# A section with its own semaphores: ending it with a NoOp on GpSimd in place of a drain

## The chip, the cores and the metric

The kernel runs on 1 core of one Trainium2 chip. The metric is device time in microseconds (us) of one execution. Kernels that are compared were run in turns on the same chip. Spans and records are of one profiled execution; a run's time is 1.7 to 1.9 us longer than its profiled span in most runs.

The views name the engines PE (TensorE's matrix products), PEld (its weight loads), DVE (VectorE), ACT (ScalarE), POOL (GpSimd) and SP (SyncE); a q after the name means the engine's queue. A semaphore is a counter that one engine increments and another waits for. A drain and a NoOp compute nothing; at the end of the section each waits for one semaphore and then increments another as its answer. They differ in what else they wait for.

## The reference, cut to what matters

One decoded token goes through attention over a long cache and, beside it, through a small feed-forward block; a gate mixes the two.

```python
def reference(A_x, A_k_cache, A_v_cache, A_wq, A_wo, B_x, B_w_gate, B_w_up, B_w_down, gate_w):
    # attention: H=32 heads, 65536 cached positions, head size 128, one query
    q = (A_x @ A_wq).reshape(...)
    p = softmax(einsum("bhqd,bhkd->bhqk", q, A_k_cache) * 128 ** -0.5)
    a = einsum("bhqk,bhkd->bhqd", p, A_v_cache).reshape(...) @ A_wo
    b = (silu(B_x @ B_w_gate) * (B_x @ B_w_up)) @ B_w_down
    g = sigmoid((A_x * gate_w).sum(-1, keepdims=True))
    return g * a + (1 - g) * b
```

K and V together are 2 x 32 x 65536 x 128 values of 2 bytes, or 1074 MB. The page below counts 1088 MB read, so nearly all of the traffic is the cache, read once.

## The kernel before

The kernel records every operation in a plan. The plan works out which semaphore values each operation must wait for. All of it is then emitted inside one section in which the kernel handles its own semaphores. The framework puts a hand-over at the end of this section: SP says that it is over, every engine answers, and SP waits for the answers.

```python
    # all that the kernel has GpSimd ("POOL") do, in the first microseconds
    # (lines for DVE between these, and the body of select, left out):
    op("POOL", "ones_b", lambda: nc.gpsimd.memset(ones_b, 1.0), writes=["ones_b"])
    select("ident", ident, ones_b, "ones_b", [[-1, P]], 1)
    select("pick", pick, ones[0:VB, 0:VB], "ones", [[-1, VB]], 1)
    op("POOL", "sel1", lambda: nc.gpsimd.memset(sel, 1.0), writes=["sel"])
    select("sel", sel, sel, "sel", [[-1, RP], [1, P]], -RP)
    # ... 32 heads: stream K and V, products on DVE, sums and P*V on PE ...
    # the last operations:
    dve("out_sb", lambda: nc.vector.scalar_tensor_tensor(...), ["m_x", "gval", "rest4"], ["out_sb"])
    dma("out", out[0, 0].rearrange("(i p) -> i p", p=P), out_sb, ["out"], ["out_sb"])
    op("SP", "end", None, reads=["out"])          # SP waits until the output has landed

    with tc.tile_critical():                       # the section with own semaphores
        # ... one semaphore for each engine and each transfer ...
        for engine in ("SP", "ACT", "POOL", "DVE"):
            for o in plan.ops:
                if o.engine == engine:
                    put(o, o.waits)                # wait, emit, increment
        # ... the same for PE, with a loop over the heads ...
```

The softmax here doesn't subtract the row's maximum and nothing guards it: scores larger than these inputs give would overflow.

## Time and profile before

The time before was 2518.3 us (median of three runs, 2518.23 to 2518.3).

| What | Before | How to read it |
|---|---|---|
| Profiled span | 2516.4 us | from the first to the last instruction |
| Read from HBM | 1088 MB, 432 GB/s | over the whole span |
| DMA slices at 90% or more | 39 of 40 | a busy transfer stream is the limit |
| GpSimd busy | 1.9 us, 9 instructions (four are of the framework) | the last is over at 2.89 us |
| From SP's "section is over" to the start of the last instruction | 1.061 us | the only stretch that the change can touch |

These lines are of the page of the kernel before: the span, the busy time of each engine with its share of the span and the number of its instructions, the busy tenths of the DMA engines and their GB/s in 40 equal slices, and the engines on the chain that ended last. The line of DMA packets gives the bytes and the mean rate.

```profile
span 2516.4 us, 15594 instructions
PE 1977.2 (79%) x9185; PEld 410.9 (16%) x5221; DVE 1268.3 (50%) x287; ACT 99.1 (4%) x402; POOL 1.9 (0%) x9
DMA  9999999999999999999999999999999999999998
GB/s 423 433 433 432 434 435 433 438 433 434 433 433 433 434 435 435 435 433 433 433 433 435 434 433 432 435 436 434 435 433 433 433 433 435 434 436 433 434 433 376
DMA packets 20478, 1088.02 MB, mean 432 GB/s; under 512 B 2282, under 2 KB 2412, under 8 KB 2668
DMA 47%; PE 39%; DVE 13%; ACT 0%; issue 0%; another core or an unknown queue 0%; SPq 0%
```

The chain names PE for 39% of the span, but the DMA engines are busy at the same time. A buffer that PE frees lets the next transfer be issued (SP, which issues the transfers, waited 64 times for PE to finish S_ps, 1418 us in all), and the transfers already queued keep the engines full meanwhile. The Trainium skill ("DMA: Bandwidth & Descriptors", section "Where 436 GB/s comes from") puts the ceiling of the ports at 435.2 GB/s. The table by stretches agrees: 434 GB/s in the long middle. (Single slices of the page reach 438, because it counts a packet in the slice where it starts. With the bytes of each packet spread over its own time, no slice of this trace is over 434.2.) The table's columns are the stretch and its length, the busy time of each engine, the granted TensorE clock, the DMA share and the GB/s.

```profile
100.00:2400.00 2300.00, 1829.38 (x7902) 364.04 (x4217) 1166.65 (x239) 88.08 (x360) 0.00 (x0) 0.91 1.00 434
2470.00:2512.00 42.00, 36.59 (x381) 13.22 (x319) 20.43 (x10) 3.48 (x13) 0.00 (x0) 0.83 0.94 401
2512.00:2516.40 4.40, 1.22 (x20) 0.76 (x19) 0.57 (x2) 0.00 (x0) 0.00 (x0) 0.50 0.00 0
```

The fifth busy figure, GpSimd's, is zero from 100 us on. The last 4.4 us move no data in bulk, and the change acts in there. The chain in order of time shows what leads up to them (start, length, what; steps of 0.05 us and less, and one of PE of 0.25 us, are left out):

```profile
2470.97 40.88 DMA slot_65<-in_A_v_cache_dram
2511.89 0.51 PE m_c L257 x13
2512.68 0.24 DVE Z L601
2512.96 0.60 PE m_x L257 x4
2513.59 0.34 DVE out_sb L613
```

After out_sb comes the store of 1 KB, issued at 2513.95; SP sees it landed at 2515.15. The hand-over follows. Drains and semaphore instructions are not counted as busy, but the view of one source line lists them. This is the line of the section (L626), with the number of instructions, their shortest, median and longest duration in ns, and the starts of the first and the last:

```profile
L626 SPq EVENT_SEMAPHORE  x3: 17/28/28, 2515.3 to 2515.6; - x3
L626 SPq NOP  x2: 13/16/18, 0.8 to 2515.6; - x2
L626 ACTq DRAIN  x1: 8/8/8, 2515.4 to 2515.4; - x1
L626 POOLq DRAIN  x1: 41/41/41, 2515.4 to 2515.4; - x1
L626 DVEq DRAIN  x1: 17/17/17, 2515.4 to 2515.4; - x1
L626 PEldq DRAIN  x1: 8/8/8, 2515.4 to 2515.4; - x1
L626 SPq DRAIN  x1: 7/7/7, 2515.4 to 2515.4; - x1
```

The raw records of the same trace give the order to the nanosecond (start and duration in ns from the first instruction; comments added):

```
2515326   17  SP      EVENT_SEMAPHORE   "the section is over"
2515364    8  ACT     DRAIN             answers
2515368   41  GpSimd  DRAIN             answers  <- what the change replaces
2515371   17  DVE     DRAIN             answers
2515372    8  PE      DRAIN             answers
2515418    7  SP      DRAIN             answers
2515476   34  GpSimd  DRAIN             the first of its three in the final barrier
2515497   28  SP      EVENT_SEMAPHORE   waits for DVE and PE
2515571   28  SP      EVENT_SEMAPHORE   waits for SP and ACT
2515643   18  SP      NOP               waits for GpSimd
2515723    7  SP      DRAIN             barrier: ready
2515787    7  SP      DRAIN             barrier: answers GpSimd
2515819   17  GpSimd  EVENT_SEMAPHORE   barrier: all have answered
2515898   17  GpSimd  EVENT_SEMAPHORE   releases the others
2515978   64  GpSimd  DRAIN             second half of the barrier
2516072   71  GpSimd  EVENT_SEMAPHORE_RANGE_CLEAR
2516100    8  PE      DRAIN             the last answer of the other engines
2516177   34  GpSimd  DRAIN
2516255   17  GpSimd  EVENT_SEMAPHORE   all have answered
2516333   17  GpSimd  EVENT_SEMAPHORE   releases the others
2516387   51  PE      EVENT_SEMAPHORE   the last instruction
```

(In the barrier, the other records of SP, ACT, DVE and PE are left out.) GpSimd has answered at 2515.409 (2515.368 + 0.041), and SP starts the instruction that waits for it at 2515.643: 234 ns to spare. A second GpSimd drain follows for the final barrier. And in the barrier's second half GpSimd comes last: the other engines have all answered by 2516.108, while GpSimd still drains at 2516.177 and releases them at 2516.333.

### The profile page before, as it was taken

To read this page: it belongs to the slowest core of one execution; us is meant where nothing else is said; L and a number is where in the kernel's file an instruction comes from. 1 tells how busy PE (TensorE), PEld (TensorE's weight loads), DVE (VectorE), ACT (ScalarE), POOL (GpSimd) and SP (SyncE) were. 2 spreads that over 40 slices of the span, in tenths; PEclk is the share of its full clock that TensorE was granted. 3 is DMA by queue.
4 is the path that set the end of the run, shared out by engine and by line. 5 is a ranking of instruction groups with operands and counts; after the bars stand their busy time and mean duration, and the time that the engine had idled before them with its cause. 6 is when DMAs were issued, how large, how long until landed. Compare 5 with 4: busy or idle time off the path is not lost.

```text
span 2516.4 us, 15594 instructions
## 1 busy us (share of the span) xinstructions
PE 1977.2 (79%) x9185; PEld 410.9 (16%) x5221; DVE 1268.3 (50%) x287; ACT 99.1 (4%) x402; POOL 1.9 (0%) x9
## 2 busy tenths in 40 slices
PE   4687877877778778778787787787877877877788
PEld 2111111111111111111111111111111111111113
DVE  3455355464553554645545546445455364464554
ACT  0000000000000000000000000000000000000000
POOL 0000000000000000000000000000000000000000
PEclk9888989989989989898898898998989989989898
DMA  9999999999999999999999999999999999999998
GB/s 423 433 433 432 434 435 433 438 433 434 433 433 433 434 435 435 435 433 433 433 433 435 434 433 432 435 436 434 435 433 433 433 433 435 434 436 433 434 433 376
DMA packets 20478, 1088.02 MB, mean 432 GB/s; under 512 B 2282, under 2 KB 2412, under 8 KB 2668
## 3 DMA queue, kind: packets, MB, share of 16 engines
q1 hardware_dynamic: 20456, 1087.78, 99.8%
q8 instruction: 12, 0.20, 0.0%
q14 instruction: 6, 0.05, 0.0%
q10 hardware_dynamic: 4, 0.00, 0.0%
HBM read 1087.77 MB, written 0.00 MB: 432 GB/s over the span
## 4 chain that ended last, share of the span: by engine, by line
DMA 47%; PE 39%; DVE 13%; ACT 0%; issue 0%; another core or an unknown queue 0%; SPq 0%
PE O_ps L257 17%; DMA slot_67<-in_A_k_cache_dram 16%; DMA slot_66<-in_A_k_cache_dram 15%; DMA slot_65<-in_A_k_cache_dram 14%; PE S_ps_103 L275 11%; PE S_ps_104 L275 9%; DVE slot_67 L344 4%; DVE slot_66 L344 4%; DVE slot_65 L344 3%; DMA slot_65<-in_A_v_cache_dram 2%; PE m_c L257 2%; DVE S_sb_82 L369 2%; PE S_ps_103 L285 1%; ACT P_sb_83 L294 0%; PE S_ps_104 L285 0%
## 5 line engine op out<-in xcount | busy, mean ns | idle before, releaser
L344 DVE TENSOR_TENSOR slot_67<-slot_67,q_bc_79 128x16384 bf16<-128x16384 bf16 (+1 forms) x28 | 208.2, 7469 | 145.4 <-DMA slot_67<-in_A_k_cache_dram 145.4
L369 DVE TENSOR_REDUCE S_sb_82<-S_ps_104 128x128 f32<-128x1024 f32 (+1 forms) x66 | 78.7, 1192 | 395.0 <-PE S_ps_104 L275 395.0
L344 DVE TENSOR_TENSOR slot_65<-slot_65,q_bc_78 128x16384 bf16<-128x16384 bf16 x22 | 190.2, 8688 | 140.5 <-DMA slot_65<-in_A_k_cache_dram 140.5
L344 DVE TENSOR_TENSOR slot_66<-slot_66,q_bc_78 128x16384 bf16<-128x16384 bf16 x22 | 190.3, 8689 | 120.1 <-DMA slot_66<-in_A_k_cache_dram 120.1
L344 DVE TENSOR_TENSOR slot_65<-slot_65,q_bc_79 128x16384 bf16<-128x16384 bf16 x20 | 172.9, 8688 | 120.0 <-DMA slot_65<-in_A_k_cache_dram 120.0
L344 DVE TENSOR_TENSOR slot_66<-slot_66,q_bc_79 128x16384 bf16<-128x16384 bf16 x20 | 172.9, 8688 | 119.2 <-DMA slot_66<-in_A_k_cache_dram 119.2
L344 DVE TENSOR_TENSOR slot_67<-slot_67,q_bc_78 128x16384 bf16<-128x16384 bf16 x20 | 172.9, 8688 | 119.2 <-DMA slot_67<-in_A_k_cache_dram 119.2
L275 PE MATMUL S_ps_103<-slot_67,ident 128*128 128x512 bf16 x680 | 193.8, 455 | 0.0
L275 PE MATMUL S_ps_103<-slot_65,ident 128*128 128x512 bf16 x651 | 186.1, 456 | 0.0
L275 PE MATMUL S_ps_103<-slot_66,ident 128*128 128x512 bf16 x651 | 183.5, 452 | 0.0
L257 PE MATMUL O_ps<-slot_67,P_sb_83 128*4 128x512 bf16 x704 | 153.7, 379 | 21.0 <-ACT P_sb_83 L294 18.3
L257 PE MATMUL O_ps<-slot_66,P_sb_84 128*4 128x512 bf16 x704 | 153.7, 379 | 19.3 <-ACT P_sb_84 L294 19.3
L257 PE MATMUL O_ps<-slot_65,P_sb_84 128*4 128x512 bf16 x640 | 139.7, 379 | 18.3 <-ACT P_sb_84 L294 18.3
L257 PE MATMUL O_ps<-slot_67,P_sb_84 128*4 128x512 bf16 x640 | 139.7, 379 | 18.3 <-ACT P_sb_84 L294 18.3
L257 PE MATMUL O_ps<-slot_65,P_sb_83 128*4 128x512 bf16 x640 | 139.7, 379 | 18.3 <-ACT P_sb_83 L294 18.3
L257 PE MATMUL O_ps<-slot_66,P_sb_83 128*4 128x512 bf16 x640 | 139.8, 379 | 17.5 <-ACT P_sb_83 L294 17.5
L275 PE MATMUL S_ps_104<-slot_67,ident 128*128 128x512 bf16 x680 | 150.7, 379 | 0.0
L275 PE MATMUL S_ps_104<-slot_66,ident 128*128 128x512 bf16 x651 | 143.9, 379 | 0.0
L275 PE MATMUL S_ps_104<-slot_65,ident 128*128 128x512 bf16 x651 | 143.9, 379 | 0.0
L285 PE MATMUL S_ps_103<-slot_65,ident 128*128 128x512 bf16 x21 | 12.8, 608 | 138.0 <-DVE slot_65 L344 138.0
L285 PE MATMUL S_ps_103<-slot_66,ident 128*128 128x512 bf16 x21 | 12.8, 608 | 131.0 <-DVE slot_66 L344 131.0
L285 PE MATMUL S_ps_103<-slot_67,ident 128*128 128x512 bf16 x24 | 13.9, 579 | 125.6 <-DVE slot_67 L344 125.6
(100 smaller groups left out, 720.4 us busy)
## 6 DMA issues: line engine op xcount, KB each, us to landing
slot_66<-in_A_k_cache_dram SPq DMA_DIRECT2D x2, 4096.0 KB, 34.9
slot_67<-in_A_k_cache_dram SPq DMA_DIRECT2D x4, 2048.0 KB, 30.3
slot_65<-in_A_wq_dram SPq DMA_DIRECT2D x1, 4096.0 KB, 12.2
slot_66<-in_A_wo_dram SPq DMA_DIRECT2D x1, 4096.0 KB, 32.4
slot_65<-in_A_v_cache_dram SPq DMA_DIRECT2D x1, 4096.0 KB, 37.1
slot_65<-in_A_v_cache_dram SPq DMA_DIRECT2D x1, 2048.0 KB, 40.3
slot_65<-in_B_w_gate_dram SPq DMA_DIRECT2D x1, 1792.0 KB, 16.0
slot_65<-in_B_w_up_dram SPq DMA_DIRECT2D x1, 1792.0 KB, 21.0
```

The costliest lines, as they stand in the source:

```text
L257: ins = nc.tensor.matmul(out_ap, lhsT=a, rhs=b, start=start and i == 0, stop=stop and i == len(pairs) - 1,)
L275: ins = nc.tensor.add_instruction(mybir.InstMatmult(name=nc.get_next_instruction_name(), engine=mybir.EngineType.PE, ins=[nc.tensor.lower_ ...
L285: ins = nc.tensor.matmul(out_ap, lhsT=a, rhs=b, start=first, stop=last)
L344: "products", lambda: nc.vector.tensor_tensor(out=w, in0=w, in1=q_rep, op=ALU.mult),
L369: lambda: nc.vector.tensor_reduce(out=S_sb[b][:, :m], in_=S_ps[r][:, :m, :], axis=AXIS.X, op=ALU.add),
```

## The change

The intent is to end the section sooner by not draining GpSimd, which has long been idle.

```diff
-    with tc.tile_critical():
+    with tc.tile_critical(no_gpsimd_drain=True):
```

The whole difference between the two programs is one instruction of GpSimd:

```diff
-Pool Drain   waits for SP's signal   increments GpSimd's answer
+Pool NoOp    waits for SP's signal   increments GpSimd's answer
```

## The prediction

> **What bounds the kernel now.** It reads 1088 MB of HBM at a mean of 432 GB/s; the page's slices show the 16 DMA engines 90% busy or more in 39 of 40. The table by stretches gives DMA shares of 0.94 to 1.00 up to 2512 us and 0.00 for the last 4.4 us. PE (1977 us busy, 79%), DVE (1268 us, 50%) and ACT (99 us) have slack. GpSimd is busy 1.9 us in all: nine instructions, the last of which starts at 2.27 us, takes 0.62 us and is over by 2.89 us. So the time is the stream of K and V, plus a tail: in the chain of waits the last piece of V lands at 2511.84 us; out_sb is done at 2513.93; the store's issue starts at 2513.95.
>
> **What the change does.** The order of instructions shows PE, DVE, ACT and SP the same. On GpSimd one Drain becomes one NoOp in the block after the section, with the same wait (SP's signal that the section is over) and the same increment; the listing hides drains, so there it looks like an added instruction. No buffer, transfer or earlier wait moves. SP still waits for the NoOp, and the final barrier keeps its own GpSimd drains.
>
> **What it costs.** The trace's records (drains are kept there, though not counted as busy) give the end, in us:
> - 2515.326 SP signals that the section is over (17 ns);
> - 2515.364 to 2515.372 ACT, GpSimd, DVE, PE start their drains: 8, 41, 17 and 8 ns; SP's at 2515.418, 7 ns;
> - 2515.497 and 2515.571 SP's waits for DVE and PE, then SP and ACT, 28 ns each;
> - 2515.643 SP's NoOp that waits for GpSimd, 18 ns;
> - 2515.723 to 2516.44 the final barrier, twice.
>
> GpSimd's drain ends at 2515.409, 0.23 us before SP starts the instruction that waits for it. A NoOp took 13 and 18 ns on SP; on GpSimd I estimate 15 to 35 ns, by the 17 to 34 ns of its semaphore and drain records, so 5 to 25 ns are saved there. SP takes about 0.075 us for each of its three waits and sets the pace, so none of it lies on the chain. GpSimd's next drain may start some 0.02 us earlier, but the barrier waits for SP, which comes at 2515.787.
>
> The Trainium skill ("PSUM — Partial Sum Buffer", section "Engine vs sequencer instructions") says that a nop waits only until earlier instructions are dispatched, a drain until the engine is fully idle. That would matter only with GpSimd work in flight at the end; this trace shows none after 2.89 us of 2516.4.
>
> **Prediction.** 2518.3 us, unchanged; best guess of the difference 0.00 us, 0.1 us at most. The range is the repeat scatter (0.07 us in three runs, 2518.14 in the profiled one) widened for other rounds: 2517.4 to 2519.1. Faster by over 2%: 0.003; within 2%: 0.994; slower by over 2%: 0.003.
>
> **What would show it.** At the section's end GpSimd has a NOP where the drain was; SP's NoOp that waits for it starts about 0.32 us after SP's signal, as before; from that signal to the last instruction's start 1.06 us, as before, within 0.05; GB/s, DMA slices and busy times unchanged.
>
> **What would make it wrong.** A GpSimd drain that holds up the others in a way the records don't show (the tail shrinks, by under 1 us); a different granted clock (now 0.908) or HBM throughput in the other runs: 0.1% of it is 2.5 us, more than the change can be; a changed layout of the program, which I don't expect because the number of instructions is the same.

## The result, and the profile after

The changed kernel took 2518.21 us (median of six runs, 2518.06 to 2518.78) and the kernel before 2518.28 us (six runs, 2518.08 to 2519.59). Ratios here are the mean time of one kernel's fast runs over that of the other's of the same rounds, so not quite the ratio of the medians. This one is 0.9999, with a 95% interval of 0.9986 to 1.0012: the same.

The page after, the same six lines:

```profile
span 2516.4 us, 15594 instructions
PE 1974.0 (78%) x9185; PEld 410.9 (16%) x5221; DVE 1268.1 (50%) x287; ACT 99.0 (4%) x402; POOL 1.9 (0%) x9
DMA  9999999999999999999999999999999999999998
GB/s 423 433 433 432 434 433 433 439 435 433 433 433 433 433 433 436 438 434 433 433 433 434 434 433 434 433 435 439 433 434 434 433 433 433 434 435 436 433 433 377
DMA packets 20478, 1088.02 MB, mean 432 GB/s; under 512 B 2282, under 2 KB 2412, under 8 KB 2668
DMA 47%; PE 39%; DVE 13%; ACT 0%; issue 0%; another core or an unknown queue 0%; SPq 0%
```

The span, the number of instructions and the DMA slices are the same. PE's busy time differs by 3 us of 1977 while the span does not, which fits that PE is not the limit. The stretches of the table agree too:

```profile
100.00:2400.00 2300.00, 1827.49 (x7910) 364.43 (x4222) 1167.18 (x239) 88.10 (x360) 0.00 (x0) 0.91 1.00 434
2512.00:2516.40 4.40, 1.16 (x20) 0.79 (x20) 0.57 (x2) 0.00 (x0) 0.00 (x0) 0.50 0.00 0
```

In the view of the section's line, GpSimd now shows a NOP of 13 ns where the drain of 41 ns was (the first four lines; the other three show the same durations as before):

```profile
L626 SPq EVENT_SEMAPHORE  x3: 17/28/28, 2515.3 to 2515.5; - x3
L626 SPq NOP  x2: 13/16/18, 0.8 to 2515.6; - x2
L626 ACTq DRAIN  x1: 8/8/8, 2515.3 to 2515.3; - x1
L626 POOLq NOP  x1: 13/13/13, 2515.3 to 2515.3; - x1
```

The raw records, each start counted in ns from SP's signal in its own trace:

```
                                           before   after
GpSimd answers: start                        42       42
GpSimd answers: duration                     41       13
GpSimd's next drain (barrier): start        150      119
GpSimd's next drain (barrier): duration      34       41
SP's NOP that waits for GpSimd: start       317      317
the last instruction: start                1061     1061
```

GpSimd is done 28 ns sooner and comes to its next drain 31 ns sooner. SP comes to its NOP at the same nanosecond, and the end is the same to the nanosecond.

### The profile page after: what moved, and what is told of

Its sections match the earlier page's. It is cut to its first block, busy times and chain, and to the rows that moved or that the text cites. A ratio compares the mean times of both kernels' runs of the same rounds, so it can differ in the third digit from the quotient of the medians.

```text
span 2516.4 us, 15594 instructions
## 1 busy us (share of the span) xinstructions
PE 1974.0 (78%) x9185; PEld 410.9 (16%) x5221; DVE 1268.1 (50%) x287; ACT 99.0 (4%) x402; POOL 1.9 (0%) x9
## 4 chain that ended last, share of the span: by engine, by line
DMA 47%; PE 39%; DVE 13%; ACT 0%; issue 0%; another core or an unknown queue 0%; SPq 0%
DMA slot<-in_A_k_cache_dram 46%; PE S_ps L275 19%; PE O_ps L257 17%; DVE slot L344 11%; DMA slot<-in_A_v_cache_dram 2%; DVE S_sb L369 2%; PE m_c L257 1%; PE S_ps L285 1%; ACT P_sb L294 0%; SPq L181 0%; PE m_sp L257 0%; PE m_x L257 0%; DVE out_sb L613 0%; DVE Z L601 0%
## 5 line engine op out<-in xcount | busy, mean ns | idle before, releaser
L344 DVE TENSOR_TENSOR slot<-slot,q_bc 128x16384 bf16<-128x16384 bf16 (+1 forms) x132 | 1107.6, 8430 | 767.3 <-DMA slot<-in_A_k_cache_dram 767.3
L275 PE MATMUL S_ps<-slot,ident 128*128 128x512 bf16 x3964 | 998.5, 416 | 0.0
L257 PE MATMUL O_ps<-slot,P_sb 128*4 128x512 bf16 x3968 | 867.8, 379 | 113.3 <-ACT P_sb L294 109.8
L257 PEld LDWEIGHTS O_ps<-slot,P_sb 128*4 128x4 bf16 x3968 | 332.4, 85 | 1055.0 <-issue 357.3
L369 DVE TENSOR_REDUCE S_sb<-S_ps 128x128 f32<-128x1024 f32 (+1 forms) x132 | 157.4, 1192 | 438.0 <-PE S_ps L275 437.7
L285 PE MATMUL S_ps<-slot,ident 128*128 128x512 bf16 x132 | 64.7, 490 | 398.7 <-DVE slot L344 398.4
L294 ACT ACTIVATE P_sb<-S_sb 128x128 bf16<-128x128 f32 (+1 forms) x132 | 40.4, 306 | 1415.6 <-DVE S_sb L369 1413.9
L294 ACT ACTIVATE O_sb<-O_ps 4x512 f32<-4x512 f32 x31 | 18.2, 587 | 437.5 <-PE O_ps L257 437.5
L257 PE MATMUL m_c<-pick,O_sb 4*128 4x1 f32 x256 | 33.5, 248 | 0.0
L257 PEld LDWEIGHTS m_c<-pick,O_sb 4*128 4x128 f32 x256 | 30.8, 186 | 13.3 <-issue 13.3
L294 ACT ACTIVATION_READ_ACCUMULATOR P_sb<-S_sb 128x1 f32 x132 | 24.6, 186 | 0.0
```

What stands on the lines that cost most here:

```text
L257: ins = nc.tensor.matmul(out_ap, lhsT=a, rhs=b, start=start and i == 0, stop=stop and i == len(pairs) - 1,)
L275: ins = nc.tensor.add_instruction(mybir.InstMatmult(name=nc.get_next_instruction_name(), engine=mybir.EngineType.PE, ins=[nc.tensor.lower_ ...
L285: ins = nc.tensor.matmul(out_ap, lhsT=a, rhs=b, start=first, stop=last)
L294: "ACT", key, lambda: nc.scalar.activation(out=out_ap, in_=in_ap, func=func, **kw),
L344: "products", lambda: nc.vector.tensor_tensor(out=w, in0=w, in1=q_rep, op=ALU.mult),
L369: lambda: nc.vector.tensor_reduce(out=S_sb[b][:, :m], in_=S_ps[r][:, :m, :], axis=AXIS.X, op=ALU.add),
```

## The experiments

Ten kernels were run. Each diff is against the kernel before unless it says otherwise. In the tables, "signal to end" is the time from SP's signal that the section is over to the start of the last instruction, from the raw records.

### Twice the same question: what a change of nothing looks like

`null` is the kernel before, unedited. `after_again` is the changed kernel once more.

> The kernel before, byte for byte, timed as if it were a new one: it measures what a change of nothing looks like. All theories: ratio 1.000, medians within 0.3 us of each other, single runs up to 1.3 us apart (as 2518.08 to 2519.59 above).

> The changed kernel once more, five rounds. Theory (the drain is off the chain, GpSimd's answer is there 0.23 us before SP looks at it): ratio 1.000, a median within 0.3 us of before, as far off as the null run is; from SP's signal to the start of the last instruction 1.061 us, as in both traces so far. Rival (the drain costs something that the records hide): a median below before by more than the null run's.

| Run | Median us (range, runs) | Ratio, 95% interval | Signal to end |
|---|---|---|---|
| before, same rounds | 2518.14 (2518.02 to 2518.40, 9) | | |
| null | 2518.22 (2518.12 to 2518.30, 5) | 1.0000, 0.9987 to 1.0014 | 1.061 us |
| after_again | 2518.48 (2518.16 to 2518.97, 5) | 1.0002, 0.9988 to 1.0016 | 1.061 us |

The median of after_again is 0.34 us above before, just over the 0.3 us expected, and in the wrong direction for a hidden cost of the drain. Two of its five runs took 2518.97 us, but their spans are 2516.5 and 2516.3 us, like the rest. So what made those two longer lies outside the span of instructions. The changed stretch itself is the same to the nanosecond in all four traces. The time of the whole run cannot show a change of this size: its interval is some 3 us to either side. The rest therefore reads the records.

### Does the drain matter if GpSimd is busy when the section ends?

GpSimd gets a memset that starts after out_sb and is still running when the section ends. It writes a buffer that nobody reads any more, so the results stay right. `late_drain` is the kernel before with it; `late_nop` is the changed kernel with it.

```diff
     op("SP", "end", None, reads=["out"])
+    ks = where["k", N - 1]
+    op("POOL", "late", lambda: nc.gpsimd.memset(slot[ks][:, :4096], 0.0),
+       reads=["out_sb"], writes=units(ks, 0, 4096))
```

> The kernel before, with one more GpSimd instruction: a memset of 128x4096 bf16 in a buffer nobody reads any more, released by out_sb. At about 1 ns for one element of a row (the memset of 32x512 took 0.51 us) it takes about 4.1 us by estimate, from 2513.97 to about 2518.1, so GpSimd is the last engine when the section ends at 2515.33. All theories: the section's drain waits for it, then SP's NoOp, then the barrier: +2.5 us over before, range 1.5 to 4.

> The same memset in the changed kernel. Theory A (the NoOp ends the section at once, but the final barrier's own GpSimd drain waits for the memset all the same): +2.3 us over before, 0.1 to 0.3 us less than late_drain; SP's NoOp stays 0.32 us after SP's signal, and the wait moves to the barrier. Theory B (without the drain nothing waits for GpSimd any more): as before, 2518.3 us, 2.5 us less than late_drain.

The time lines show the memset in both; it took 3.51 us and not the 4.1 that was estimated. The first line is late_drain:

```profile
2514.14 3.51 POOL L622 MEMSET slot<- 128x4096 bf16 x1 [2511.26 <-DVE out_sb L613]
```

and this one late_nop:

```profile
2514.12 3.51 POOL L622 MEMSET slot<- 128x4096 bf16 x1 [2511.24 <-DVE out_sb L613]
```

What GpSimd does at the section's line (L626) and in the final barrier (L704), in late_drain:

```profile
L626 POOLq DRAIN  x1: 2196/2196/2196, 2515.5 to 2515.5; - x1
L704 POOLq DRAIN  x3: 34/41/64, 2517.8 to 2518.3; - x3
```

and in late_nop:

```profile
L626 POOLq NOP  x1: 13/13/13, 2515.5 to 2515.5; - x1
L704 POOLq DRAIN  x3: 34/70/2119, 2515.6 to 2518.1; - x3
```

The drain that takes 2196 ns at the section's end becomes a drain of 2119 ns in the barrier. The barrier still waits for the memset; the wait only comes one step later.

| Run | Median us (range, 4 runs) | Signal to SP's NOP | Signal to end | End of memset to end |
|---|---|---|---|---|
| late_drain | 2520.14 (2520.09 to 2520.25) | 2.264 us | 3.008 us | 0.837 us |
| late_nop | 2520.16 (2520.08 to 2520.23) | 0.317 us | 2.858 us | 0.686 us |

The busy GpSimd costs 2.0 us in both (2520.14 and 2520.16, less 2518.14 of the same rounds). Theory B, that without the drain nothing waits for GpSimd, fell: it wanted 2518.3. Theory A held. Of the whole wait the NoOp saves 0.151 us (0.837 less 0.686): SP's hand-over runs while the memset still does, and not after it. Even this does not show in the medians, whose ranges overlap.

The pair also tests a sentence that the prediction drew on. The Trainium skill ("PSUM — Partial Sum Buffer", section "Engine vs sequencer instructions") says that a nop waits only until earlier instructions are dispatched, and a drain until the engine is fully idle. The traces agree for GpSimd: with the memset running, the NOP took 13 ns, as beside an idle engine, and the drain 2196 ns.

### What one drain costs, and one NoOp

32 more instructions are put on GpSimd, released when the output has landed. `many_drains` adds drains to the kernel before; `many_nops` adds NoOps to the changed kernel.

```diff
+        count = ctx.enter_context(nc.semaphore("s_count"))
+        nc.gpsimd.wait_ge(sems["out"], 16)
+        for _ in range(32):
+            nc.gpsimd.drain().then_inc(count, 1)      # many_nops: nc.gpsimd.nop(hint="n")
         def pe(a, b):
```

> The kernel before, with 32 more GpSimd drains, each with a semaphore increment, released when the output has landed, at about 2515.1 us in the trace of before. GpSimd is idle then, so this measures the disputed cost by itself, made long enough to lie on the chain. If one takes its place every 0.06 to 0.09 us (estimate from 41 ns of the record plus fetching), they end at 2517.0 to 2518.0, against 2515.41 for the drain now: +1.4 to +2.4 us on the time. Rival (a drain of an idle GpSimd stalls it far longer than its record): +5 us or more.

> The changed kernel with 32 GpSimd NoOps in the same place, each with the same increment. Theory: 15 to 40 ns less for each than a drain, so 0.5 to 1.3 us less than many_drains in all; a 32nd of the difference is what the change could be worth if GpSimd's answer were on the chain.

The view of the added line, first of many_drains:

```profile
L648 POOLq DRAIN  x32: 34/34/41, 2515.3 to 2518.3; - x32
```

then of many_nops:

```profile
L648 POOLq NOP  x32: 13/13/13, 2515.1 to 2517.5; - x32
```

| Run | Median us (range, 4 runs) | Record of one | From one start to the next | First one to the last instruction |
|---|---|---|---|---|
| before, same rounds | 2518.31 (2518.05 to 2518.43, 7 runs) | | | |
| many_drains | 2520.85 (2520.74 to 2520.94) | 34 ns | 95.8 ns | 3.906 us |
| many_nops | 2520.33 (2520.11 to 2520.37) | 13 ns | 76.6 ns | 3.256 us |

(The step between starts is worked out from the records after the first: 2.875 us for 30 drains, 2.298 us for 30 NoOps.) A drain of an idle GpSimd takes its place every 95.8 ns. The guess of 60 to 90 was low, and so the added 2.54 us (2520.85 less 2518.31) are a little over the expected 1.4 to 2.4. The rival, a stall of 5 us or more, fell. A NoOp is 19.2 ns faster, inside the expected 15 to 40. So the change could be worth about 0.02 to 0.03 us if GpSimd's answer were on the chain: 19 ns by this row of instructions, 28 ns by the end of the one answer in the traces of before and after. The medians agree within their scatter: 0.52 us apart, where 33 exchanged instructions (32 and the section's own) make 0.63 us.

### How much GpSimd may be late

Fewer drains of the same kind, one look each, to find where they begin to cost.

> As many_drains, with 3 drains for 32. In many_drains the first drain starts 0.161 us before SP's signal, the second 0.108 us after the first, the others every 0.096 us, the section's own drain 0.114 us after the last, and SP's NoOp 0.060 us after that. Theory (SP's waits set the pace, GpSimd's answer has some 0.21 us to spare): the section's drain starts 0.318 us after the first one, SP could go on at 0.378 us, but comes by itself only at 0.478 us (0.317 us after its signal): from SP's signal to the start of the last instruction 1.06 us, as without the drains. Rival (every drain of GpSimd on its way adds to the end): 0.16 us or more longer, 1.22 us.

> As many_drains, with 8. Theory: the section's drain starts 0.80 us after the first one, SP's NoOp at 0.86 us and not at 0.478 us: the answer is late by 0.38 us and the same 0.38 us is added, 1.44 us from SP's signal to the start of the last instruction. Rival (the end takes up GpSimd's delay elsewhere): 1.06 us.

| Run | us (1 run) | Section's drain: start after the signal | Its end to SP's NOP | Signal to SP's NOP | Signal to end |
|---|---|---|---|---|---|
| null (no extra drain) | 2518.22 (median of 5) | 0.041 us | 0.234 us | 0.316 us | 1.061 us |
| drains_3 | 2518.16 | 0.156 us | 0.127 us | 0.317 us | 1.066 us |
| drains_8 | 2518.66 | 0.635 us | 0.027 us | 0.696 us | 1.445 us |

SP's NOP and GpSimd's drain at the section's line, in drains_3 (SP's signal is at 2515.328):

```profile
L626 SPq NOP  x2: 13/16/18, 0.8 to 2515.6; - x2
L626 POOLq DRAIN  x1: 34/34/34, 2515.5 to 2515.5; - x1
```

and in drains_8 (signal at 2515.455):

```profile
L626 SPq NOP  x2: 13/16/18, 0.8 to 2516.2; - x2
L626 POOLq DRAIN  x1: 34/34/34, 2516.1 to 2516.1; - x1
```

With three drains in its way, GpSimd's answer ends 0.108 us later than in null (0.156 + 0.034 us after the signal, against 0.041 + 0.041), and SP comes to its NOP at the same time as ever. (The 5 ns more at the end arise later: up to GpSimd's drain at 0.652 us the two traces agree within 2 ns, and its next instruction is 4 ns later.) With eight, SP waits: its NOP starts 27 ns after GpSimd's drain has ended, and the end is 0.384 us later (1.445 less 1.061). Both match the expectation, 1.06 and 1.44 us; the single run times, 0.05 and 0.55 us above the one run of before beside them (2518.11), go the same way. So an answer reaches SP some 26 to 27 ns after the record ends (26 in late_drain and many_drains, 27 in many_nops and drains_8), and of the 234 ns between GpSimd's answer and SP's NOP in the kernel before, about 208 are true slack. The change makes this slack 28 ns larger.

### Is the drain short only because GpSimd issues no transfer here?

The load of the gate row, 1 KB, is issued by GpSimd and not by ACT, in the kernel before (`swq_drain`) and in the changed kernel (`swq_nop`).

```diff
-    dma("gw", gw_row, gate_w.unsqueeze(0), ["gw_row"], engine="ACT")
+    dma("gw", gw_row, gate_w.unsqueeze(0), ["gw_row"], engine="POOL")
```

> The kernel before, with the load of the gate row (1 KB) issued by GpSimd and not by ACT. It lands within the first 20 us. Question: is the drain short only because GpSimd issues no transfer in this kernel? Theory: the transfer is long done at the end, the section's drain takes 0.1 us at most, and the tail from SP's signal stays at 1.06 us. Rival: a GpSimd that has issued a transfer takes over 0.3 us to drain, and the tail grows by as much.

> The same in the changed kernel. Theory: same as swq_drain within 0.1 us from SP's signal to the end. Rival: the section's NoOp is short, but the barrier's drains have to do what the section's drain did, so the tail is long here too and the change saves one drain of two or three.

GpSimd at the section's line and in the barrier, in swq_drain:

```profile
L626 POOLq DRAIN  x1: 125/125/125, 2515.1 to 2515.1; - x1
L704 POOLq DRAIN  x3: 34/40/71, 2515.3 to 2515.9; - x3
```

and in swq_nop:

```profile
L626 POOLq NOP  x1: 13/13/13, 2515.3 to 2515.3; - x1
L704 POOLq DRAIN  x3: 40/71/125, 2515.4 to 2516.2; - x3
```

One small transfer, over for about 2.5 ms, makes the first drain after it three times as long: 125 ns for 41 in swq_drain. That is over the 0.1 us that the theory allowed and well under the 0.3 us of the rival. The 125 ns go to whichever drain comes first: the section's in one kernel, the barrier's in the other. From the signal to the end both took nearly the same, 1.070 and 1.075 us. The 9 and 14 ns over 1.061 arise in the barrier's second half, where GpSimd's records are longer by a few ns (its two drains 71 and 34 ns in swq_drain, 71 and 40 in swq_nop, against 64 and 34 before, and its clearing of semaphores 73 against 71): there nothing hides them. The medians are 2518.02 and 2518.16 us against 2518.31 of the same rounds. Why the drain grows is not settled by these two runs, and a kernel with GpSimd transfers still in flight at the end was not tried.

No experiment points to a version that beats both kernels. GpSimd's answer to SP is off the chain. Its work in the final barrier is on it, from 0.493 to 1.007 us after the signal in the kernel before, but the change does not touch that, and the whole stretch is 1.06 us of 2516.4.

## Why the prediction was right

- **The limit is the stream from HBM.** Right: the DMA slices and the mean of 432 GB/s are the same after. The best a change in the last microsecond can do is 1.06 us, less than the 1.5 us between the fastest and the slowest of the six runs of before.
- **One instruction changes, none moves.** Right: by engine, operation and line, the two traces have the same instructions but for one NOP for one drain.
- **GpSimd's part gets 5 to 25 ns shorter.** Slightly off: the NOP took 13 ns where 15 to 35 were estimated, so the record is 28 ns shorter. The estimate leaned on other kinds of GpSimd records (17 to 34 ns); SP's NOP of the same trace (13 to 18 ns) would have been the better guide. Counted from one instruction to the next, the saving is 19 ns (many_drains and many_nops). GpSimd's next drain came 31 ns sooner, not 20.
- **None of it is on the chain, because SP sets the pace.** Right, and shown as a cause: SP's NOP starts 0.317 us after the signal with the drain, with the NoOp and with three more drains, and is late only when GpSimd's answer comes later than that (drains_8). The 0.23 us to spare are 0.21 once the way of the answer is taken off.
- **It would matter only with GpSimd work in flight.** Right in direction, but smaller than it sounds: the barrier drains GpSimd once more, so 2.0 us of waiting stay and only 0.151 us are saved (late_drain and late_nop). The prediction named the barrier's own drains, but did not draw this conclusion.
- **The time.** 2518.21 us measured, 2518.3 predicted, inside 2517.4 to 2519.1. This alone says little: a gain of 0.8 us would have fallen inside the range too. It is the records that bear the mechanism out.

## What to carry to other kernels

Before taking away a wait or a drain, ask who reads its answer and when: an engine that answers before it is asked can be made faster without any gain. Ask it step by step: GpSimd is off the chain in this hand-over and on it in the barrier that follows. Look also for the next barrier on the way, for it may wait for the same thing, and then the change only moves the wait. When the stopwatch has an interval of 3 us and the change is worth 0.02, count from one event to the next in the records, and multiply the cost (32 times here) to measure it.

## What the Trainium skill lacked or had wrong

- No page gives the cost of a GpSimd drain or NoOp from one instruction to the next (for the record of a drain see the fourth point). Here a drain is 34 to 64 ns in the record on an idle GpSimd, but 95.8 ns from one drain to the next; a NoOp is 13 ns in the record and 76.6 ns from one to the next. This belongs on "GPSIMD Engine Reference".
- No page says that an earlier transfer issued by GpSimd lengthens its next drain: 125 ns for 41 here, with a 1 KB load about 2.5 ms before.
- "Perfetto Trace Analysis" (section "Sequencer-only Instruction (DRAIN, etc)") says that the profile shows only the execution of such an instruction, and neither the wait before it nor the way of its semaphore after it. The traces agree, but the page has no number for the way: here 26 to 27 ns from the end of GpSimd's record to the start of the SP instruction that waited for it.
- "VectorE: DVE Perf Modes" (section "The DRAIN you can't avoid") calls the drains of the runtime's own start and end a constant of about 12 ns on all five engines. The drains at the end of this program, which may not be the ones it means, are 7 to 17 ns on SP, ACT, DVE and PE, but 34 to 64 ns on an idle GpSimd.
- "DMA: Bandwidth & Descriptors" (section "Where 436 GB/s comes from") says without a condition that transfers from HBM are bound by about 358 GB/s; the same page, below the measured sizes further up, gives this figure for the case that both cores of the HBM domain stream, so only the sentence lacks the condition. This core's loads, with nothing in these runs to show what the other cores did, ran at 434 GB/s for 2300 us, at the ceiling that the page gives for the ports.
